# Decode block: gate and up products one step earlier, the MLP's last weights behind the fourth K tile, and half of one head's output weights on 64 partitions

## The chip, the cores and the metric

The kernel runs on one core of one Trainium2 chip; the other cores stand idle. The time is device microseconds of that core for one execution. The core has five engines with instruction streams of their own: TensorE (PE, matmuls; PEld is its weight load), VectorE (DVE), ScalarE (ACT), GpSimd (POOL) and SyncE (SP). SP does no arithmetic here: it issues the transfers from HBM into the on-chip memory (SBUF, 128 partitions), and 16 DMA engines carry them out. A transfer that SP cannot issue yet, because its buffer is still being read, holds up every transfer behind it in SP's stream.

## The reference

One token of a decoder block for a batch of two, in float32: grouped-query attention over a cached context, multiplied by a gated MLP.

```python
# B, D, Hq, Hkv, Sk, Dh, F = 2, 512, 32, 8, 32768, 128, 1792
xn = layernorm(x)                                   # x is (2, 1, 512)
q  = (xn @ wq) as (B, Hq, 1, Dh)
scores = q . k_cache * Dh**-0.5                     # 4 query heads share one K/V head
o  = softmax(scores) . v_cache
s  = o.reshape(B, 1, Hq*Dh) @ wo                    # wo is (4096, 512)
gate, up = xn @ W_gate, xn @ W_up                   # (512, 1792) each
g  = silu((gate * (gate > 0) * up) @ W_down)        # W_down is (1792, 512)
out = x + s * g
```

Each of the two caches holds 2 x 8 x 32768 x 128 floats (268 MB); all weights together are 27.8 MB. Everything is read once.

## The kernel before

**Tiles and steps.** A group is one batch row and one K/V head: 16 groups, ordered head by head with the two batch rows next to each other. A group's 32768 keys are four tiles of 8192 keys (4 MB of K, 4 MB of V each), so there are 64 K tiles, called k0 to k63 here, and 64 steps `s`. In step `s` DVE transposes K tile `s` in four parts (`k_transpose`, tiles named `kts`, buffers from `ktpool`, five of them), PE forms the scores (`scores`, tile `s_...`), and in step `s + 1` DVE copies them out of the accumulators and takes the maximum (`take_scores`, tile `sc`). After a group's fourth tile come the group's maximum (`tile_maximum`, `maximum`) and the exponentials on ACT. Four steps behind the scores, PE reorders the exponentials (`weights`), DVE transposes them (`take_weights`), and in odd steps PE multiplies two tiles with V (`values`, into `o_ps`). Eight steps after a group began, `take_o` and `finish_group` normalise its result; once the second batch row of a head is there, `finish_group` turns the two rows into columns (tile `ots`) by small matmuls that pick rows out of `ob`. Behind the last step `project_near` multiplies the heads 0 to 4 with their part of `wo`, and `project_far` the heads 5 to 7, adds both, multiplies with the MLP's result and adds `x`.

**The MLP.** Its products lie inside the first steps: `mlp_gu` (gate, then up: `ps_g`, `ps_u`) on PE, `mlp_take` and `mlp_h` on DVE, `mlp_down` (`ps_d`) on PE, and the sigmoid-weighted unit on ACT.

**Buffers and the transfer queue.** All large loads go through `load`, that is, through SP's stream, in the order in which the code issues them. Two pools of SBUF receive them. `ring` has two buffers of 32 KB per partition; K tiles take turns in them, and at the end two V tiles and the output weights do. A K tile's buffer is free when its fourth transpose is done. `wide` has one buffer of 64 KB per partition; in turn it holds `wq`, the gate and up weights (`wgu`), the down weights (`wd`), and then pairs of V tiles (`load_vv`, called vv0, vv2, ... here by their first tile). It is free when the last matmul that reads it is done: for `wq` the query projection, for `wgu` the up product, for `wd` the down product, for a V pair the values of both tiles.

**What sets the order.** The tables `extra` (PE work behind a step), `taken` (DVE work within a step) and `ahead` (loads issued behind a step) say in which step a piece stands; the loop over `s` writes each step out, and `pin` ties PE's and DVE's instructions to the order written, while SP issues in the order of the code. Before the loop stand k0, k1, the query projection, and the gate and up weights.

Of the kernel before, what the change touches and what calls it, by code (L numbers as in the profile page):

```python
# [8 lines left out]
F32 = mybir.dt.float32  # L9
# [4 lines left out]
P = 128  # L14
Q = 32
NC = 4
NR = 16
TK = P * NC * NR
SLOTS = 2
NEAR = 5  # L20
ALIGN = 512


@with_exitstack
def kernel(
# [12 lines left out]
    nc = tc.nc  # L38
    B, HKV, SK, DH = kc.shape
    D = x.shape[2]  # L40
# [15 lines left out]
    const = ctx.enter_context(tc.tile_pool(name="const", bufs=1))  # L56
    ktpool = ctx.enter_context(tc.tile_pool(name="ktpool", bufs=5))
    spool = ctx.enter_context(tc.tile_pool(name="spool", bufs=NU + 2))
    work = ctx.enter_context(tc.tile_pool(name="work", bufs=2))
# [25 lines left out]
    n = 1  # L85
# [27 lines left out]
    ots = const.tile([P, HKV, 2, 2, 32], F32, name="ots")  # L113
    nc.vector.memset(ots, 0.0)
    ob = const.tile([64, DH], F32, name="ob")
    nc.vector.memset(ob, 0.0)
    fold = const.tile([P, 32], F32, name="fold")
    nc.vector.reduce_sum(fold, ident.rearrange("p (k m) -> p m k", m=32), axis=AX.X)
    gy = const.tile([P, P], F32, name="gy")
# [4 lines left out]
    KT, VT, ST, KTS, LS, MX, WO = {}, {}, {}, {}, {}, {}, {}  # L124
    SPS, PR, PW = {}, {}, {}

    def load(dst, src):
        nc.sync.dma_start(dst, src)

    def group(g):  # L130
        return g % B, g // B

    def rows_of(src, t, n):
        b, hk = group(t // NU)
        lo = (t % NU) // 2 * 2 * TK
        rows = src[b, hk, lo : lo + 2 * TK, :]
        if n == 2:
            return rows.rearrange("(p r) d -> p (r d)", p=P)
        return rows.rearrange("(p i r) d -> i p (r d)", i=2, p=P)[t % 2]

    def load_one(src, t, name):
        dst = ring.tile([P, NC, NR, DH], F32, tag="r", align_bytes=ALIGN, name=f"{name}_{t}")
        load(dst.rearrange("p c r d -> p (c r d)"), rows_of(src, t, 1))
        return dst
# [7 lines left out]
    def load_vv(t):  # L152
        dst = wide.tile([P, 2, NC, NR, DH], F32, tag="w", align_bytes=ALIGN, name=f"v_{t}")
        load(dst.rearrange("p i c r d -> p (i c r d)"), rows_of(vc, t, 2))
        for i in range(2):
            VT[t + i] = dst[:, i]

    def load_wo(lo, hi):
        w = ring.tile([P, 4, 2, 2, D], F32, tag="r", align_bytes=ALIGN, name=f"wo_{lo}")
        r = REP * DH  # L160
        for hk in range(lo, hi):
            WO[hk] = w[:, hk - lo]
            dst = WO[hk].rearrange("p c i d -> p c (i d)")
            rows = wo[hk * r : (hk + 1) * r, :].rearrange("(c p i) d -> p c (i d)", c=2, i=2)
            if hk < HKV - 1:
                load(dst, rows)
                continue
            load(dst[:, 0], rows[:, 0])
            for i in range(2):
                load(dst[:, 1, i * D : (i + 1) * D], rows[:, 1, i * D : (i + 1) * D])  # L170


    QW = wq.shape[1] // 2
    wqt = wide.tile([P, NKC, 2, QW], F32, tag="w", align_bytes=ALIGN, name="wq")
    load(
# [52 lines left out]
    def load_gu():  # L228
        t = wide.tile([P, 2, NKC, F], F32, tag="w", align_bytes=ALIGN, name="wgu")
        for n, (which, w) in enumerate((("g", wg), ("u", wu))):  # L230
            load(
                t[:, n].rearrange("p k f -> p (k f)"),
                w.rearrange("(p k) f -> p (k f)", k=NKC),
            )
            for k in range(NKC):
                mlp[which, k] = t[:, n, k, :]
# [31 lines left out]
    def load_d():  # L268
        t = wide.tile([P, FI, D], F32, tag="w", align_bytes=ALIGN, name="wd")
        load(t.rearrange("p i d -> p (i d)"), wd.rearrange("(p i) d -> p (i d)", p=P))  # L270
        for i in range(FI):
            mlp["d", i] = t[:, i, :]
# [13 lines left out]


    def k_transpose(t, c):
        part = ktpool.tile([P, NR, 4, Q], F32, tag="kt", name=f"kts_{t}_{c}")
        nc.vector.transpose(  # L290
            part.rearrange("p r e k -> p (r e k)"), KT[t][:, c].rearrange("p r d -> p (r d)")
        )
        KTS.setdefault(t, []).append(part)
# [113 lines left out]
    def finish_group(g):  # L407
        b, hk = group(g)
        if b == 0:
            PO[hk] = ps_m.tile([P, 512], F32, tag="m", name=f"po_{hk}")  # L410
        po, o = PO[hk], OS.pop(g)
        mine = slice(32 * b, 32 * b + REP)
        nc.tensor.matmul(  # L413
            po[mine, :], head, o.rearrange("p c d -> p (c d)"), start=True, stop=True
        )
        nc.vector.reduce_sum(  # L416
            ob[mine, :], po[mine, :].rearrange("p (c d) -> p d c", c=NC), axis=AX.X
        )
        if b < B - 1:
            return  # L420
        PO.pop(hk)
        ob2 = ob.rearrange("p (q i) -> p i q", i=2)
        pick = ident.rearrange("p (b c r) -> p r c b", b=4, r=2)
        for r in range(2):
            for i in range(2):
                nc.tensor.matmul(  # L426
                    po[64 * r : 64 * r + 64, 256 + i * 4 : 260 + i * 4],
                    ob2[:, i, :],
                    pick[:64, r, :2, :B],
                    start=True,  # L430
                    stop=True,
                )
        nc.vector.tensor_copy(
            ots[:, hk, :, :, :B],
            po[:, 256:264].rearrange("p (i c b) -> p c i b", i=2, c=2),
        )

    PY = {}
# [1 line left out]
    def project_near(hks):  # L440
        if not PY:
            PY["near"] = ps_s.tile([P, 512], F32, tag="s", name="py_near")
        for hk in hks:
            w = WO.pop(hk)
            for k in range(4):
                nc.tensor.matmul(  # L446
                    PY["near"][32 * k : 32 * k + 32, :],
                    ots[:, hk, k // 2, k % 2, :],
                    w[:, k // 2, k % 2, :],
                    start=(hk == 0),  # L450
                    stop=(hk == NEAR - 1),
                )
        if hks[-1] == NEAR - 1:
            PY["sb"] = work.tile([P, 4, P], F32, tag="os", name="py_sb")
            nc.vector.tensor_copy(PY["sb"].rearrange("p c n -> p (c n)"), PY["near"])

    def project_far(hks):
        py = ps_s.tile([P, 512], F32, tag="s", name="py")
        parts = [(fold, PY["sb"].rearrange("p c n -> p (c n)"))]
        for hk in hks:  # L460
            w = WO.pop(hk)
            parts += [(ots[:, hk, k // 2, k % 2, :], w[:, k // 2, k % 2, :]) for k in range(4)]
        for n, (o, w) in enumerate(parts):
            for c in range(4):
                nc.tensor.matmul(  # L465
                    py[32 * c : 32 * c + 32, :P],
                    o,
                    w[:, c * P : (c + 1) * P],
                    start=(n == 0),
                    stop=(n == len(parts) - 1),  # L470
                )
        nc.vector.tensor_mul(gy, py[:, :P], gy)
        nc.vector.tensor_add(gy, gy, xy)

    extra, taken, ahead = {}, {}, {}

    def at(where, s, f, *a):
        where.setdefault(s, []).append((f, a))

    END = NK + NU  # L480
    at(ahead, 1, load_d)
    for s in range(NK - 2):
        at(ahead, s, load_k, s + 2)
        if s % 2 and s >= 3:
            at(ahead, s, load_vv, s - 3)
    at(ahead, NK - 2, load_v, NK - 4)
    at(ahead, NK - 1, load_v, NK - 3)
    at(ahead, NK - 1, load_vv, NK - 2)
    at(ahead, NK + 1, load_wo, 0, 4)
    at(ahead, NK + 1, load_wo, 4, HKV)  # L490
    at(extra, 1, mlp_gu, "g")
    at(extra, 1, mlp_gu, "u")
    at(taken, 2, mlp_take, "g")
    at(taken, 2, mlp_take, "u")
    at(taken, 2, mlp_h)
# [28 lines left out]
    for s in range(END + 1):  # L524
        done = s // NU - 2 if s % NU == 0 and s >= 2 * NU else None
        full = s // NU - 1 if 0 < s <= NK and s % NU == 0 else None
        w = s - NU
        if s < NK:
            k_transpose(s, 0)
# [8 lines left out]
        if s < NK:  # L538
            k_transpose(s, 1)
        if full is not None:  # L540
            maximum(full)
        if s < NK:
            k_transpose(s, 2)
        if s == END:
            project_near(range(4))
        if done is not None:
            finish_group(done)
# [7 lines left out]
        if s == END:  # L555
            project_near(range(4, NEAR))
            project_far(range(NEAR, HKV))
        if s % 2 and w > 0:
# [10 lines left out]
    rows = gy.rearrange("(c q) n -> q c n", q=32)  # L569
# [33 lines left out]
```

## Time and profile before

| | |
|---|---|
| median of 3 runs | 1330.86 us (1330.72 to 1330.94) |
| the profiled execution's own time | 1330.93 us |
| its span, first to last instruction | 1329.1 us |
| PE, PEld, DVE, ACT busy | 908.2, 216.8, 707.1, 52.1 us |
| HBM read | 564.67 MB, 425 GB/s over the span |
| mean granted TensorE clock | 0.836 |

The profile is one execution. Its page gives the busy time of each engine, the span in 40 slices of 33 us with the share of time in which the 16 DMA engines were busy, the chain of work that ended last, and the costliest groups of instructions. Further views are the timeline (instructions with start and duration in us and, in brackets, how long the engine had been idle and what released it), tables by stretches of time, and who waited for whom. A DMA row of the timeline (SPq) is the issue on SP, not the transfer; a row that joins several issues has the start of the first.

### The profile page before, as it was taken

To read this page: it belongs to the slowest core of one execution; us is meant where nothing else is said; L and a number is where in the kernel's file an instruction comes from. 1 tells how busy PE (TensorE), PEld (TensorE's weight loads), DVE (VectorE), ACT (ScalarE), POOL (GpSimd) and SP (SyncE) were. 2 spreads that over 40 slices of the span, in tenths; PEclk is the share of its full clock that TensorE was granted. 3 is DMA by queue.
4 is the path that set the end of the run, shared out by engine and by line. 5 is a ranking of instruction groups with operands and counts; after the bars stand their busy time and mean duration, and the time that the engine had idled before them with its cause. 6 is when DMAs were issued, how large, how long until landed. Compare 5 with 4: busy or idle time off the path is not lost.

```text
span 1329.1 us, 10685 instructions
## 1 busy us (share of the span) xinstructions
PE 908.2 (68%) x4736; PEld 216.8 (16%) x4736; DVE 707.1 (53%) x667; ACT 52.1 (4%) x136; POOL 0.7 (0%) x6
## 2 busy tenths in 40 slices
PE   3586667776775776767568676757767676776775
PEld 1121111121111111111111111112111111111112
DVE  3848445466644546656454665545466554546610
ACT  0001000000000000000000000000000000000000
POOL 0000000000000000000000000000000000000000
PEclk9799788878878887878897778888889777987887
DMA  9979999999999999999999999999999999999997
GB/s 411 427 314 411 440 415 423 440 427 439 436 438 427 432 427 436 431 442 438 426 428 431 435 432 438 432 440 424 430 432 437 439 428 438 430 427 431 444 429 307
DMA packets 16962, 565.36 MB, mean 425 GB/s; under 512 B 1794, under 2 KB 1810, under 8 KB 3988
## 3 DMA queue, kind: packets, MB, share of 16 engines
q1 hardware_dynamic: 16888, 564.67, 98.6%
q8 instruction: 37, 0.61, 0.2%
q14 instruction: 9, 0.07, 0.0%
q10 hardware_dynamic: 28, 0.01, 0.0%
HBM read 564.67 MB, written 0.00 MB: 425 GB/s over the span
## 4 chain that ended last, share of the span: by engine, by line
DMA 66%; DVE 26%; PE 7%; issue 1%; DVEq 0%
DMA k<-in_A_k_cache_dram 60%; DVE kts L290 21%; DMA v<-in_A_v_cache_dram 5%; PE s L302 2%; PE o_ps L374 2%; DMA wq<-in_A_wq_dram 2%; DVE sc L316 1%; DVE os L396 1%; DVE ob L416 1%; PE pr L344 1%; PE pq L201 1%; DVE qt L220 0%; PE po L426 0%; PE py_near L446 0%; PE py L465 0%
## 5 line engine op out<-in xcount | busy, mean ns | idle before, releaser
L290 DVE STREAM_TRANSPOSE kts<-k 128x2048 f32<-128x2048 f32 x256 | 578.0, 2287 | 462.8 <-DMA k<-in_A_k_cache_dram 462.8
L302 PE MATMUL s<-kts,qt 128*32 128x512 f32 x2048 | 490.0, 729 | 186.6 <-DVE kts L290 183.3
L374 PE MATMUL o_ps<-v,sc 128*16 128x512 f32 x2048 | 258.7, 646 | 80.3 <-DMA v<-in_A_v_cache_dram 80.3
L302 PEld LDWEIGHTS s<-kts,qt 128*32 128x32 f32 x2048 | 97.0, 128 | 579.0 <-DVE kts L290 322.2
L374 PEld LDWEIGHTS o_ps<-v,sc 128*16 128x16 f32 x2048 | 62.4, 102 | 255.8 <-issue 167.1
L352 ACT ACTIVATE sc<-sc,nb 128x512 f32<-128x512 f32 x64 | 45.4, 710 | 1130.4 <-DVE nb L348 1130.4
L358 PE MATMUL pt<-sc,perm 128*128 128x512 f32 x128 | 85.4, 757 | 1.3 <-ACT sc L352 1.3
L316 DVE TENSOR_SCALAR_CACHE_REDUCE sc<-s 128x512 f32<-128x512 f32 x64 | 43.1, 673 | 58.9 <-PE s L302 58.9
L330 PE MATMUL pr<-ident,m 128*1 128x128 f32 x16 | 5.2, 327 | 79.3 <-DVE m L328 79.3
L367 DVE STREAM_TRANSPOSE sc<-pt 128x512 f32<-128x512 f32 x64 | 43.3, 676 | 12.7 <-PE pt L358 12.4
L344 PE MATMUL pr<-negone,mrow 1*128 1x1 f32 x32 | 8.9, 344 | 33.4 <-DVE mrow L341 33.4
L358 PEld LDWEIGHTS pt<-sc,perm 128*128 128x128 f32 x128 | 22.0, 215 | 54.1 <-issue 39.2
L413 PE MATMUL po<-os,head 128*4 128x512 f32 x32 | 28.2, 982 | 0.0
L394 DVE RECIPROCAL rl<-pl 128x1 f32<-128x1 f32 x16 | 2.6, 164 | 26.4 <-PE pl L389 26.4
L330 PEld LDWEIGHTS pr<-ident,m 128*1 128x1 f32 x16 | 1.3, 79 | 94.0 <-DVE m L328 92.1
L396 DVE SCALAR_TENSOR_TENSOR os<-o_ps,rl,own 128x512 f32<-128x512 f32 x16 | 12.0, 751 | 8.3 <-PE o_ps L374 6.8
L344 PEld LDWEIGHTS pr<-negone,mrow 1*128 1x128 f32 x32 | 7.5, 290 | 37.4 <-DVE mrow L341 37.4
L201 PE MATMUL pq<-wq,xt 128*32 128x512 f32 x64 | 8.8, 715 | 6.7 <-DMA wq<-in_A_wq_dram 6.7
L416 DVE TENSOR_REDUCE ob<-po 4x128 f32<-4x512 f32 x16 | 10.6, 662 | 4.5 <-PE po L413 4.3
L277 PE MATMUL ps_d<-wd,ht 128*32 128x512 f32 x28 | 12.2, 592 | 0.0
L352 ACT ACTIVATION_READ_ACCUMULATOR sc<-sc,nb 128x1 f32 x64 | 11.9, 186 | 0.0
L426 PE MATMUL po<-ident,ob 64*64 64x4 f32 x64 | 4.6, 244 | 10.5 <-DVE ob L416 10.5
(74 smaller groups left out, 107.6 us busy)
## 6 DMA issues: line engine op xcount, KB each, us to landing
k<-in_A_k_cache_dram SPq DMA_DIRECT2D x64, 4096.0 KB, 26.7
v<-in_A_v_cache_dram SPq DMA_DIRECT2D x2, 4096.0 KB, 29.5
wo<-in_A_wo_dram SPq DMA_DIRECT2D x7, 1024.0 KB, 17.7
wgu<-in_B_W_gate_dram SPq DMA_DIRECT2D x1, 3584.0 KB, 19.9
wgu<-in_B_W_up_dram SPq DMA_DIRECT2D x1, 3584.0 KB
wd<-in_B_W_down_dram SPq DMA_DIRECT2D x1, 3584.0 KB
wo<-in_A_wo_dram SPq DMA_DIRECT2D x1, 512.0 KB
wo<-in_A_wo_dram SPq DMA_DIRECT2D x2, 256.0 KB
```

Of the source, the lines that this page charges most:

```text
L201: nc.tensor.matmul(pq[half][32 * c : 32 * c + 32, :], xn[:, k, :], wqt[:, k, half, c * 512 : (c + 1) * 512], start=(k == 0), stop=(k == NK ...
L290: nc.vector.transpose(part.rearrange("p r e k -> p (r e k)"), KT[t][:, c].rearrange("p r d -> p (r d)"))
L302: nc.tensor.matmul(ps[Q * c : Q * c + Q, :], qt[:, b, hk, e, :], kts[c][:, :, e, :], start=(e == 0), stop=(e == 3),)
L316: nc.vector.tensor_scalar(ST[t].rearrange("p r m -> p (r m)"), SPS.pop(t), SCALE, None, op0=ALU.mult, op1=ALU.max, accum_out=MX[g][:, u : ...
L344: nc.tensor.matmul(pr[:, 256:257], mrow.rearrange("o c k h -> o (c k h)"), negone, start=True, stop=True)
L352: nc.scalar.activation(st, st, AF.Exp, bias=nbias, scale=1.0, accum_out=LS[g][:, u : u + 1])
L358: nc.tensor.matmul(PW[t], perm.rearrange("p k c h -> p (k c h)"), ST[t].rearrange("p r m -> p (r m)"), start=True, stop=True,)
L367: nc.vector.transpose(ST[t].rearrange("p r m -> p (r m)"), PW.pop(t))
L374: nc.tensor.matmul(ops[g % 2][a : a + NC * REP, :, :], w[:, r, : NC * REP], v[:, :, r, :], start=(u == 0 and r < 4), stop=(u == NU - 1 and ...
L396: nc.vector.scalar_tensor_tensor(OS[g], ops[g % 2], rl, own.unsqueeze(2).to_broadcast([P, NC, DH]), op0=ALU.mult, op1=ALU.mult,)
L413: nc.tensor.matmul(po[mine, :], head, o.rearrange("p c d -> p (c d)"), start=True, stop=True)
L416: nc.vector.reduce_sum(ob[mine, :], po[mine, :].rearrange("p (c d) -> p d c", c=NC), axis=AX.X)
```

## The change

Three edits and their consequences:

- `mlp_gu` for gate and up stands behind step 0 instead of step 1, so PE has both products ahead of the scores of k1.
- `load_d` (the down weights) stays in step 1, but behind the load of k3 instead of ahead of it. What followed in SP's stream keeps its order.
- Head 6's output weights (`LOW = 6`), 1 MB, are loaded in three transfers instead of one: the first half as before into 128 partitions, the second half as two transfers of 256 KB into the partitions 0 to 31 and 32 to 63 of a `ktpool` buffer (`wo_low`, 8 KB per partition). `finish_group` for that head makes a rearranged copy of `ob` (`obl`) and eight small matmuls into a new tile `otl` (64 partitions); `project_far` uses four products of 64 partitions there in place of two of 128. The `ktpool` tiles get an alignment of 512 bytes.

```diff
@@ load_wo
+            if hk == LOW:
+                load(dst[:, 0], rows[:, 0])
+                WO["low"] = ktpool.tile([P, 4, D], F32, tag="kt", align_bytes=ALIGN, name="wo_low")
+                flat = WO["low"].rearrange("p j d -> p (j d)")
+                for h in range(2):
+                    a = hk * r + (2 + h) * P
+                    load(
+                        flat[32 * h : 32 * h + 32, :],
+                        wo[a : a + P, :].rearrange("(a e j) d -> e a (j d)", a=4, e=8),
+                    )
+                continue
             if hk < HKV - 1:
                 load(dst, rows)
@@ k_transpose
-        part = ktpool.tile([P, NR, 4, Q], F32, tag="kt", name=f"kts_{t}_{c}")
+        part = ktpool.tile([P, NR, 4, Q], F32, tag="kt", align_bytes=ALIGN, name=f"kts_{t}_{c}")
@@ finish_group
+        n = 1 if hk == LOW else 2
...
+        if hk != LOW:
+            return
+        obl = work.tile([P, NC, DH], F32, tag="os", name="obl")[:64, 0].rearrange(
+            "p (j x) -> p j x", j=4
+        )
+        nc.vector.tensor_copy(
+            obl.rearrange("p j (e a) -> p j e a", a=4),
+            ob.rearrange("p (a e j) -> p j e a", a=4, e=8),
+        )
+        for h in range(2):
+            for j in range(4):
+                nc.tensor.matmul(
+                    po[32 * h : 32 * h + 32, 320 + j * B : 320 + (j + 1) * B],
+                    obl[:, j, :],
+                    pick[:64, h, 1, :B],
+                    start=True,
+                    stop=True,
+                )
+        nc.vector.tensor_copy(
+            otl[:, :, :B], po[:64, 320 : 320 + 4 * B].rearrange("p (j b) -> p j b", j=4)
+        )
@@ project_far
-            parts += [(ots[:, hk, k // 2, k % 2, :], w[:, k // 2, k % 2, :]) for k in range(4)]
+            n = 2 if hk == LOW else 4
+            parts += [(ots[:, hk, k // 2, k % 2, :], w[:, k // 2, k % 2, :]) for k in range(n)]
+            if hk == LOW:
+                parts += [(otl[:, j, :], WO["low"][:64, j, :]) for j in range(4)]
@@ tables of the loop
-    at(ahead, 1, load_d)
     for s in range(NK - 2):
         at(ahead, s, load_k, s + 2)
+        if s == 1:
+            at(ahead, s, load_d)
...
-    at(extra, 1, mlp_gu, "g")
-    at(extra, 1, mlp_gu, "u")
+    at(extra, 0, mlp_gu, "g")
+    at(extra, 0, mlp_gu, "u")
```

**Where it moves instructions.** On SP, early in the program, before: `k_306` is k2, `k_372`, `k_428` and `k_457` are k3, k4 and k5, `wd` the down weights, `v_459` the pair vv0.

```order
L128 DMA wgu<-in_B_W_up_dram 128x7168
L128 DMA k_306<-in_A_k_cache_dram 128x8192
L128 DMA wd<-in_B_W_down_dram 128x7168
L128 DMA k_372<-in_A_k_cache_dram 128x8192
L128 DMA k_428<-in_A_k_cache_dram 128x8192
L128 DMA k_457<-in_A_k_cache_dram 128x8192
L128 DMA v_459<-in_A_v_cache_dram 128x16384
```

The same place in the changed kernel, where `k_342`, `k_372`, `k_430` and `k_459` are k2 to k5 and `v_461` is vv0:

```order
L131 DMA wgu<-in_B_W_up_dram 128x7168
L131 DMA k_342<-in_A_k_cache_dram 128x8192
L131 DMA k_372<-in_A_k_cache_dram 128x8192
L131 DMA wd<-in_B_W_down_dram 128x7168
L131 DMA k_430<-in_A_k_cache_dram 128x8192
L131 DMA k_459<-in_A_k_cache_dram 128x8192
L131 DMA v_461<-in_A_v_cache_dram 128x16384
```

k3 and `wd` have changed places. On PE, around the gate and up products, before (`s_319` are the scores of k1, `s_392` those of k2, `kts_0_...` to `kts_3_...` the four transposed parts of a tile):

```order
L302 MATMUL s_319<-kts_2_315,qt 32x512
L302 MATMUL s_319<-kts_3_317,qt 32x512
L242 MATMUL ps_g<-wgu,xt 32x448 x16
L242 MATMUL ps_u<-wgu,xt 32x448 x16
L302 MATMUL s_392<-kts_0_374,qt 32x512
L302 MATMUL s_392<-kts_1_386,qt 32x512
```

In the changed kernel, where `s_291` are the scores of k0 and `s_355` those of k1:

```order
L316 MATMUL s_291<-kts_2_287,qt 32x512
L316 MATMUL s_291<-kts_3_289,qt 32x512
L256 MATMUL ps_g<-wgu,xt 32x448 x16
L256 MATMUL ps_u<-wgu,xt 32x448 x16
L316 MATMUL s_355<-kts_0_344,qt 32x512
L316 MATMUL s_355<-kts_1_349,qt 32x512
```

Both products now stand ahead of the scores of k1. On PE at the program's end, before (`py_near` and `py` are the accumulators of the two projections):

```order
L446 MATMUL py_near<-wo_3889,ots 32x512 x16
L413 MATMUL po_3848<-os_3945,head 4x512
L426 MATMUL po_3848<-ident,ob 64x4 x4
L446 MATMUL py_near<-wo_3894,ots 32x512 x4
L465 MATMUL py<-py_sb,fold 32x128 x4
L465 MATMUL py<-wo_3894,ots 32x128 x48
```

And in the changed kernel:

```order
L482 MATMUL py_near<-wo_3902,ots 32x512 x16
L427 MATMUL po_3861<-os_3961,head 4x512
L441 MATMUL po_3861<-ident,ob 64x4 x4
L482 MATMUL py_near<-wo_3907,ots 32x512 x4
L504 MATMUL py<-py_sb,fold 32x128 x4
L504 MATMUL py<-wo_3907,ots 32x128 x24
L504 MATMUL py<-wo_low,otl 32x128 x16
L504 MATMUL py<-wo_3907,ots 32x128 x16
```

The far projection has 56 products of weights instead of 48; the trace counts each float32 product as two instructions, 96 before.

More of the change, by code (lines that the diff above doesn't have):

```diff
@@ L20 @@
 NEAR = 5
+LOW = 6
 ALIGN = 512
@@ L116 @@
     nc.vector.memset(ob, 0.0)
+    otl = const.tile([64, 4, 32], F32, name="otl")
+    nc.vector.memset(otl, 0.0)
     fold = const.tile([P, 32], F32, name="fold")
@@ L426, in finish_group @@
                 nc.tensor.matmul(
-                    po[64 * r : 64 * r + 64, 256 + i * 4 : 260 + i * 4],
+                    po[64 * r : 64 * r + 64, 256 + i * n * B : 256 + (i + 1) * n * B],
                     ob2[:, i, :],
-                    pick[:64, r, :2, :B],
+                    pick[:64, r, :n, :B],
                     start=True,
@@ L433, in finish_group @@
         nc.vector.tensor_copy(
-            ots[:, hk, :, :, :B],
-            po[:, 256:264].rearrange("p (i c b) -> p c i b", i=2, c=2),
+            ots[:, hk, :n, :, :B],
+            po[:, 256 : 256 + 2 * n * B].rearrange("p (i c b) -> p c i b", i=2, c=n),
+        )
[19 more added lines that the diff above has]
+            otl[:, :, :B], po[:64, 320 : 320 + 4 * B].rearrange("p (j b) -> p j b", j=4)
         )
```

## The prediction

> **What bounds the kernel now.** I read the page first: busy times, the DMA and GB/s rows of the slices, and the queue that carries the loads.
>
> ```profile
> PE 908.2 (68%) x4736; PEld 216.8 (16%) x4736; DVE 707.1 (53%) x667; ACT 52.1 (4%) x136; POOL 0.7 (0%) x6
> DMA  9979999999999999999999999999999999999997
> GB/s 411 427 314 411 440 415 423 440 427 439 436 438 427 432 427 436 431 442 438 426 428 431 435 432 438 432 440 424 430 432 437 439 428 438 430 427 431 444 429 307
> q1 hardware_dynamic: 16888, 564.67, 98.6%
> k<-in_A_k_cache_dram SPq DMA_DIRECT2D x64, 4096.0 KB, 26.7
> wd<-in_B_W_down_dram SPq DMA_DIRECT2D x1, 3584.0 KB
> ```
>
> No compute engine is near full, and the DMA engines are: 98.6% of their time goes into the load queue. Only two slices fall below 411 GB/s, the third (66 to 100 us) and the last. A K tile waits 26.7 us from issue to landing. Next I read the table by stretches; its last columns are the granted clock, the DMA share and GB/s.
>
> ```profile
> 60.00:65.00 5.00, 3.83 (x4) 0.36 (x4) 5.00 (x3) 0.00 (x0) 0.00 (x0) 0.54 0.99 426
> 65.00:70.00 5.00, 4.89 (x40) 1.56 (x44) 0.41 (x2) 0.00 (x0) 0.00 (x0) 0.78 0.50 216
> 70.00:75.00 5.00, 5.00 (x58) 2.87 (x50) 3.17 (x4) 0.00 (x0) 0.00 (x0) 1.00 0.01 3
> 75.00:80.00 5.00, 0.79 (x5) 0.00 (x0) 4.11 (x5) 0.00 (x0) 0.00 (x0) 1.00 0.73 264
> 105.00:110.00 5.00, 3.62 (x26) 0.90 (x26) 3.60 (x3) 0.00 (x0) 0.00 (x0) 1.00 0.61 216
> 160.00:1240.00 1080.00, 752.38 (x3838) 175.10 (x3830) 587.81 (x508) 41.01 (x112) 0.00 (x0) 0.83 1.00 433
> ```
>
> From 160 to 1240 us the share is 1.00 at 433 GB/s: in the long middle nothing but bytes sets the pace, and each microsecond in which the DMA engines stand idle is added to the end. They stood idle 2.5 + 4.95 + 1.35 = 8.8 us around 68 to 77 us and 1.95 us around 106 us, together 10.75 us. The timeline of SP's issues, of DVE and of PE says why.
>
> ```profile
> 51.23 0.33 SPq L128 DMA_DIRECT2D k<-in_A_k_cache_dram  x1
> 57.75 0.69 DVE L316 TENSOR_SCALAR_CACHE_REDUCE sc<-s 128x512 f32<-128x512 f32 x1 [4.36 <-PE s L302]
> 58.37 6.69 DVE L290 STREAM_TRANSPOSE kts<-k 128x2048 f32<-128x2048 f32 x3
> 65.11 4.23 PE L302 MATMUL s<-kts,qt 128*32 128x512 f32 x25 [0.28 <-DVE kts L290]
> 69.65 2.31 DVE L290 STREAM_TRANSPOSE kts<-k 128x2048 f32<-128x2048 f32 x1 [4.59 <-DMA k<-in_A_k_cache_dram]
> 71.88 0.65 DVE L316 TENSOR_SCALAR_CACHE_REDUCE sc<-s 128x512 f32<-128x512 f32 x1
> 72.52 2.52 PE L242 MATMUL ps_u<-wgu,xt 128*32 128x448 f32 x24
> 75.82 0.33 SPq L128 DMA_DIRECT2D wd<-in_B_W_down_dram  x1
> 75.83 0.62 DVE L253 COPY sb_u<-ps_u 128x448 f32<-128x448 f32 x1 [2.38 <-PE ps_u L242]
> 76.25 30.16 SPq L128 DMA_DIRECT2D k<-in_A_k_cache_dram  x3
> 78.54 6.66 DVE L290 STREAM_TRANSPOSE kts<-k 128x2048 f32<-128x2048 f32 x3
> 88.29 11.75 PE L277 MATMUL ps_d<-wd,ht 128*32 128x512 f32 x27
> 106.50 0.38 SPq L128 DMA_DIRECT2D v<-in_A_v_cache_dram  x1
> 109.77 0.69 DVE L316 TENSOR_SCALAR_CACHE_REDUCE sc<-s 128x512 f32<-128x512 f32 x1 [1.17 <-PE s L302]
> 118.25 11.41 SPq L128 DMA_DIRECT2D k<-in_A_k_cache_dram  x2
> 138.79 8.79 PE L374 MATMUL o_ps<-v,sc 128*16 128x512 f32 x64 [5.80 <-DMA v<-in_A_v_cache_dram]
> 147.65 0.33 SPq L128 DMA_DIRECT2D v<-in_A_v_cache_dram  x1
> 148.49 2.31 DVE L290 STREAM_TRANSPOSE kts<-k 128x2048 f32<-128x2048 f32 x1 [18.58 <-DMA k<-in_A_k_cache_dram]
> 1197.67 2.31 DVE L290 STREAM_TRANSPOSE kts<-k 128x2048 f32<-128x2048 f32 x1 [16.91 <-DMA k<-in_A_k_cache_dram]
> ```
>
> k2 is issued at 51.23 and is there at 69.65. The next issue, `wd`, goes out at 75.82, when the up product has freed the wide buffer, and k3 stands behind it (76.25) although its own buffer was free at 58.37 + 6.69 = 65.06, when k1's transposes ended. So the queue ran dry. It ran dry again at 106: the third issue of the row at 76.25 is k5, which ended that row at 106.4 and waited for k3's transposes, late because k3 was late.
>
> **What the gaps are worth.** k6 reaches DVE at 148.49, k60 at 1197.67. In between lie 27 periods of two K tiles and a V pair, 108 tiles: 1049.18 / 108 = 9.715 us a tile with the queue never empty. Between k2 (69.65) and k6 (148.49) the queue carried `wd` (3584/4096 = 0.875 tile), k3 to k6 and a V pair, 6.875 tiles, which take 66.79 us at that pace. It took 78.84. The excess is 12.05 us; the idle shares explain 10.75 of it, and the rest I put down to restarting from empty.
>
> **Edits to the loads and the MLP.** With k3 first, SP issues it at 65.1, 4.5 us before k2 lands, and no longer waits for PE there. What is queued behind, at one tile per 9.715 us from 69.65: k3 lands at 79.4, `wd` at 87.9, k4 at 97.6, k5 at 107.3, vv0 at 126.7, k6 at 136.5, k7 at 146.2. Each next issue must come before its predecessor lands.
>
> - `wd` waits for the up product. PE is free for gate and up when the scores of k0 are out (57.75); the up weights are there one tile before k2, by 59.9. The 24 matmuls of the row at 72.52 took 2.52 us at clock 1.00, so all 64 take 6.7 us, at the 0.54 of the stretch 60 to 65 us 12.4. Done at 64 to 70; needed by 79.4. Queued behind on PE are k1's scores, on SP k4.
> - k4 waits for k2's transposes. DVE does the first by 71.96, then takes k1's scores (0.65). These are ready 4.23 us after k1's last transpose by the row at 65.11, at 69.3; if PE is held by the MLP until 70.1 and all 32 matmuls follow, at 75.6. Then come the five MLP steps, 2.7 us from 75.83 to 78.54 and 0.6 for the gate copy, without the 2.38 us wait, and three transposes (6.66): issue at 82.6 to 86.2, against 87.9. Before it was 85.2.
> - k5 waits for k3's transposes: on DVE from 82.6, the first done by 84.9, k2's scores ready 4.2 us after k2's last transpose and taken by 87.5, three more transposes: 94.2, against 97.6.
> - vv0 waits for the down product, 12.2 us (11.75 for 27 of its 28 instructions) from `wd`'s landing: 100.1, against 107.3. At this place PE now waits for `wd`, about 2 us, and k3's scores stand behind it.
> - k6: k3's scores end at about 104.3; before, k6 left 8.48 us after that point (109.77 to 118.25): 112.8, against 126.7. vv2 follows the values of vv0, 8.8 us after its landing: 135.6, against 146.2. That is the 10 us of backlog it had before (147.65).
>
> Every margin is positive, the smallest 1.7 to 5.3 us (k4) and 3.4 us (k5). I take the whole 12.05 us. A transfer needs a moment from issue to its first bytes, and the scores too may run at a low clock, so that up to 2 us can come back at k4.
>
> **Head 6, in the middle.** In step 60 come two DVE copies, eight small products (16 instructions) and a wait of DVE for PE ahead of the last transpose.
>
> ```profile
> 1207.91 0.60 PE L426 MATMUL po<-ident,ob 64*64 64x4 f32 x8 [1.38 <-DVE ob L416]
> 1208.57 0.17 DVE L433 COPY ots<-po 128x8 f32<-128x8 f32 x1 [0.71 <-PE po L426]
> 1210.99 12.88 SPq L128 DMA_DIRECT2D k<-in_A_k_cache_dram  x2
> v<-in_A_v_cache_dram SPq DMA_DIRECT2D x31, 30.3
> ```
>
> Twice the 0.60 us, since there are twice as many, less the overlap, and two copies of 0.17 to 0.3: an estimate of 1.2 us by which k62's issue (1210.99) is later. The cover is the backlog: a K tile lands 26.7 us after its issue, 17 of them behind others, a V pair 30.3 for 19.4 of its own. Cost zero; 1.2 us if there were no backlog. The memset of `otl` lies in DVE's wait for `x` at the start, and the alignment adds no instruction: zero.
>
> **Head 6, at the end.** All of it hangs on the last V pair.
>
> ```profile
> 1305.21 5.83 PE L374 MATMUL o_ps<-v,sc 128*16 128x512 f32 x32 [12.16 <-DMA v<-in_A_v_cache_dram]
> 1322.43 2.94 PE L465 MATMUL py<-wo,ots 128*32 128x128 f32 x96
> 1324.94 0.16 PEld L465 LDWEIGHTS py<-wo,ots 128*32 128x32 f32 x8 [0.19 <-DMA wo<-in_A_wo_dram]
> 1320.00:1322.00 2.00, 1.37 (x16) 0.44 (x16) 0.73 (x2) 0.00 (x0) 0.00 (x0) 1.00 0.57 235
> 1283.33 28.47 SPq L128 DMA_DIRECT2D wo<-in_A_wo_dram  x10
> ```
>
> From the landing of the last V pair PE runs to the end with one wait for weights, 0.19 us. Sixteen more instructions at 2.94/96 = 31 ns cost 0.5 us, and the wait can vanish: +0.3. The share of 0.57 says that about nine of the sixteen DMA engines are still busy when the others are done, so the last weights belong to late engines. If the 512 KB move from late engines to early ones, the last landing comes earlier and nothing more is gained than the 0.19. If they move onto the late ones, they take 2.4 us at half of 433 GB/s instead of 1.2, the last landing is 1.2 us later and the end with it. So -0.2 to +1.2. I take +0.3, since the instructions are certain and no row tells the late engines from the early. SP's two more issues cost nothing: ten went out by 1311.8, and two more at the 0.33 us of a single issue are out before the weights ahead of them have moved.
>
> [...]
>
> **Sum.** The profiled execution took 1330.93 us, 0.07 above the median. 1330.93 - 12.05 + 0.3 = 1319.2 us.
>
> **The rivals.**
> - Part of the gap comes back: k4, k5 or vv0 misses its moment, because PE with the MLP in front is late under a low clock. For it speaks the 0.54 just where the products now stand; against it that DVE loses its 2.38 us wait. Price 2 to 5 us: 1321 to 1324.
> [...]
> - Slower: not bytes but the turnaround of the two ring buffers sets the steady pace. Then the early gain is swallowed by a later wait, and what head 6 adds stays: 1.2 in step 60, 0.5 for instructions, 1.2 for the landing, 2.9 in all, 1333.8. It decides once the backlog at an issue is under 1.2 us; the 1.00 share over 1080 us speaks against it.
> - The reorder does nothing, because k3 is not ready to go before the up product either: about 1331. Against it stands 65.06 from the transposes.
>
> **How the numbers follow.** Forecast with its tail bounds, 1318.6 to 1320.5, including the rival of the eight late engines (0.15 of it): 0.77. Part of the gap back: 0.16. Slower: 0.03. No effect: 0.03. The rest, 0.01, is a gain beyond the excess. To hold 8 in 10 the range goes from 1318.0, a little under the bound of the excess (1330.93 - 12.05 - 0.2 = 1318.7), to 1322.5, halfway into the partial case. About 0.2% (2.7 us) is what a measurement of this kernel can tell from no change: faster 0.94, same 0.03, slower 0.03.
>
> **What would show it.** Right: DMA share near 1.00 in all stretches from 65 to 130 us, k3 issued at 65, `wd` at 64 to 70, k6 on DVE at about 136.5 instead of 148.5, the last V pair's values 12 us earlier, and the same length from there to the end but for 0.3. Wrong: a stretch with a low share between 80 and 110 us (k4, k5 or vv0 late), a pace above 9.715 us a tile later on, or a longer wait for `wo` in the far projection.

## The result and the profile after

The changed kernel takes 1320.59 us in the median of 6 runs (1319.75 to 1323.00), the kernel before 1330.9 (1330.07 to 1332.61): a ratio of 0.9923 with an interval of 0.9911 to 0.9936. So it is faster, by 0.8%. The profiled execution took 1319.75 us, and its span is 1318.0 us. The forecast was 1319.2, in a range of 1318.0 to 1322.5.

From the page of the changed kernel, the DMA row of the slices and the load queue:

```profile
DMA  9999999999999999999999999999999999999997
q1 hardware_dynamic: 16840, 564.67, 99.3%
```

The third slice is full (7 before) and the queue takes 99.3% of the DMA engines' time (98.6% before) for the same 564.67 MB. The table by stretches, with the granted clock, the DMA share and GB/s at the end (a packet counts in the stretch in which it starts, so a short stretch can show a share above 1):

```profile
65.00:78.00 13.00, 5.28 (x28) 0.92 (x20) 7.98 (x9) 0.00 (x0) 0.00 (x0) 0.79 1.01 434
90.00:100.00 10.00, 10.00 (x30) 2.57 (x29) 5.97 (x3) 0.00 (x0) 0.00 (x0) 1.00 0.99 406
104.00:109.00 5.00, 0.90 (x4) 0.62 (x4) 4.26 (x8) 0.92 (x3) 0.00 (x0) 0.76 1.11 478
65.00:130.00 65.00, 46.96 (x207) 11.11 (x203) 43.08 (x35) 5.28 (x13) 0.00 (x0) 0.84 1.00 426
160.00:1240.00 1080.00, 747.65 (x3860) 173.24 (x3852) 588.94 (x511) 41.01 (x112) 0.00 (x0) 0.84 1.00 433
```

Both gaps are closed, and none has opened around 95 us, where the queue, which now runs some 10 us earlier, could have run dry. The middle runs as before. The timeline of the changed kernel, SP's issues first, then rows of PE and DVE:

```profile
52.17 12.90 SPq L131 DMA_DIRECT2D k<-in_A_k_cache_dram  x2
65.25 0.33 SPq L131 DMA_DIRECT2D wd<-in_B_W_down_dram  x1
82.69 11.35 SPq L131 DMA_DIRECT2D k<-in_A_k_cache_dram  x2
100.31 0.33 SPq L131 DMA_DIRECT2D v<-in_A_v_cache_dram  x1
112.49 11.76 SPq L131 DMA_DIRECT2D k<-in_A_k_cache_dram  x2
135.98 0.33 SPq L131 DMA_DIRECT2D v<-in_A_v_cache_dram  x1
60.23 3.21 PE L256 MATMUL ps_u<-wgu,xt 128*32 128x448 f32 x32
86.38 0.69 DVE L330 TENSOR_SCALAR_CACHE_REDUCE sc<-s 128x512 f32<-128x512 f32 x1 [1.52 <-PE s L316]
88.10 11.75 PE L291 MATMUL ps_d<-wd,ht 128*32 128x512 f32 x27 [1.76 <-DMA wd<-in_B_W_down_dram]
97.72 2.31 DVE L304 STREAM_TRANSPOSE kts<-k 128x2048 f32<-128x2048 f32 x1 [4.03 <-DMA k<-in_A_k_cache_dram]
137.06 2.31 DVE L304 STREAM_TRANSPOSE kts<-k 128x2048 f32<-128x2048 f32 x1 [12.57 <-DMA k<-in_A_k_cache_dram]
1187.02 2.31 DVE L304 STREAM_TRANSPOSE kts<-k 128x2048 f32<-128x2048 f32 x1 [16.03 <-DMA k<-in_A_k_cache_dram]
```

In the first row two issues are grouped, k2 at 52.17 and k3, which ends the group at 65.07; `wd` follows at once, since the up product ends at 63.4. In the same way k5 goes out at the end of the row at 82.69, at 94.0, and k4 reaches DVE at 97.72. k6 reaches DVE at 137.06, 11.43 us earlier than before (148.49), k60 at 1187.02, 10.65 earlier. The pace between them is (1187.02 - 137.06) / 108 = 9.722 us a tile, against 9.715.

The end of the program, on PE, PE's weight loads and DVE's part of step 60:

```profile
1197.93 0.16 DVE L448 COPY ots<-po 128x4 f32<-128x4 f32 x1 [0.71 <-PE po L441]
1199.17 0.16 DVE L470 COPY otl<-po 64x8 f32<-64x8 f32 x1 [0.91 <-PE po L463]
1293.52 5.73 PE L388 MATMUL o_ps<-v,sc 128*16 128x512 f32 x32 [12.26 <-DMA v<-in_A_v_cache_dram]
1310.64 1.49 PE L504 MATMUL py<-wo,ots 128*32 128x128 f32 x48
1312.06 1.08 PE L504 MATMUL py<-wo_low,otl 64*32 64x128 f32 x32
1313.07 1.40 PE L504 MATMUL py<-wo,ots 128*32 128x128 f32 x32
1314.04 0.16 PEld L504 LDWEIGHTS py<-wo,ots 128*32 128x32 f32 x8 [0.38 <-DMA wo<-in_A_wo_dram]
```

The last V pair's product starts 11.69 us earlier than before (1305.21). From there to the end of the span it is 24.48 us, against 23.9 before. So 11.7 us were gained up to the last V pair and 0.6 went back at the end; the two profiled executions differ by 11.2.

### The profile page after: what moved, and what is told of

It reads as the page before. It is cut to its first block, busy times and chain, and to the rows that moved or that the text cites. A ratio compares the mean times of both kernels' runs of the same rounds, so it can differ in the third digit from the quotient of the medians.

```text
span 1318.0 us, 10755 instructions
## 1 busy us (share of the span) xinstructions
PE 899.1 (68%) x4768; PEld 214.6 (16%) x4768; DVE 707.3 (54%) x670; ACT 52.1 (4%) x136; POOL 0.7 (0%) x6
## 3 DMA queue, kind: packets, MB, share of 16 engines
q1 hardware_dynamic: 16840, 564.67, 99.3%
HBM read 564.67 MB, written 0.00 MB: 428 GB/s over the span
## 4 chain that ended last, share of the span: by engine, by line
DMA 67%; DVE 25%; PE 6%; issue 1%; SPq 0%; DVEq 0%; ACT 0%; ACTq 0%
DMA k<-in_A_k_cache_dram 59%; DVE kts L304 21%; DMA wo<-in_A_wo_dram 3%; DMA v<-in_A_v_cache_dram 2%; DMA wd<-in_B_W_down_dram 2%; DMA wq<-in_A_wq_dram 2%; PE s L316 1%; DVE sc L330 1%; PE o_ps L388 1%; PE ps_d L291 1%; DVE os L410 1%; PE pr L358 1%; PE pq L215 1%; DVE ob L430 1%; DVE qt L234 0%
## 5 line engine op out<-in xcount | busy, mean ns | idle before, releaser
L316 PE MATMUL s<-kts,qt 128*32 128x512 f32 x2048 | 483.5, 721 | 190.3 <-DVE kts L304 187.1
L388 PE MATMUL o_ps<-v,sc 128*16 128x512 f32 x2048 | 253.3, 634 | 77.8 <-DMA v<-in_A_v_cache_dram 77.8
L441 PE MATMUL po<-ident,ob 64*64 64x4 f32 (+1 forms) x64 | 4.6, 244 | 10.5 <-DVE ob L430 10.5
```

The costliest lines, as they stand in the source:

```text
L316: nc.tensor.matmul(ps[Q * c : Q * c + Q, :], qt[:, b, hk, e, :], kts[c][:, :, e, :], start=(e == 0), stop=(e == 3),)
L388: nc.tensor.matmul(ops[g % 2][a : a + NC * REP, :, :], w[:, r, : NC * REP], v[:, :, r, :], start=(u == 0 and r < 4), stop=(u == NU - 1 and ...
```

## The experiments

**The theory:** the gain is the closing of the two gaps of the load queue, by the two edits together; head 6 adds nothing to it. The first four runs have each edit of the start alone, both of them without head 6, and head 6 alone.

*k3 ahead of `wd`, and nothing else.* On the kernel before:

```
-    at(ahead, 1, load_d)
     for s in range(NK - 2):
         at(ahead, s, load_k, s + 2)
+        if s == 1:
+            at(ahead, s, load_d)
```

> The kernel before with one edit: k3's load ahead of the down weights; gate and up stay behind the scores of k1. Theory (the transfer queue only has to hold something at all times): k3 goes out at 65, the down weights still at 76 when the up product is done, which is 3 us before k3 lands, so the queue never runs dry; k4 as before at 85, ahead of the landing of the down weights at 88. About 1319 us, the whole 11 to 12 us of the change. Rival 1 (the early products do the work, because they free the wide buffer): k3 alone ahead gains only its own tile, about 1327 to 1329. Rival 2 (each edit brings a share): about 1325.

Measured: 1323.01 us, ratio 0.9935 (0.9920 to 0.9949). The theory's 1319 is missed by 4 us. The table by stretches of this kernel and its timeline:

```profile
65.00:78.00 13.00, 11.06 (x92) 4.37 (x84) 5.37 (x8) 0.00 (x0) 0.00 (x0) 0.87 1.02 434
90.00:100.00 10.00, 10.00 (x26) 2.53 (x23) 7.87 (x6) 0.00 (x0) 0.00 (x0) 1.00 0.89 354
76.09 0.33 SPq L128 DMA_DIRECT2D wd<-in_B_W_down_dram  x1
85.49 13.05 SPq L128 DMA_DIRECT2D k<-in_A_k_cache_dram  x2
90.87 0.69 DVE L316 TENSOR_SCALAR_CACHE_REDUCE sc<-s 128x512 f32<-128x512 f32 x1 [3.22 <-PE s L302]
99.44 2.31 DVE L290 STREAM_TRANSPOSE kts<-k 128x2048 f32<-128x2048 f32 x1 [1.26 <-DMA k<-in_A_k_cache_dram]
```

The first gap is closed. The second stays, only smaller and earlier: k5 goes out at the end of its row, 85.49 + 13.05 = 98.5, still ahead of k4's arrival on DVE (99.44), and yet the queue runs dry. The packet records of this trace (each DMA packet with its start, duration and size) show why. Fifteen of the sixteen engines had run out of k4's packets between 97.0 and 98.9 us, and the first packets of k5 come at 99.2, 0.95 us after its issue began at 98.2. With the MLP products still behind k1's scores, k2's transposes are done 2.8 us later than in the changed kernel (k4 at 85.49, not 82.69), and DVE waits 3.22 us for k2's scores instead of 1.52, so that k5 is 4.5 us later.

*The products early, and nothing else.*

```
-    at(extra, 1, mlp_gu, "g")
-    at(extra, 1, mlp_gu, "u")
+    at(extra, 0, mlp_gu, "g")
+    at(extra, 0, mlp_gu, "u")
```

> The kernel before with the other edit: gate and up behind the scores of k0; the down weights stay ahead of k3. Theory: the down weights go out at about 64, k3 at 65, so the gap at 68 to 77 us closes here too; but k3 lands one transfer later (88 instead of 79), its transposes end at about 97, just when k4 has landed, so that the gap of 1.7 us idle and its restart, about 2.3 us, stays: 1321 us. Rival 1 (the early products do all): 1319. Rival 2 (each edit a share): about 1325.

Measured: 1322.62 us, ratio 0.9934 (0.9918 to 0.9951). The theory had the right gap and 1321 us, 1.6 too few. Its stretches and SP's issues:

```profile
65.00:78.00 13.00, 4.81 (x24) 0.79 (x16) 8.14 (x9) 0.00 (x0) 0.00 (x0) 0.76 1.02 437
90.00:100.00 10.00, 10.00 (x47) 3.28 (x47) 9.74 (x7) 2.34 (x5) 0.00 (x0) 1.00 0.71 285
63.35 0.33 SPq L128 DMA_DIRECT2D wd<-in_B_W_down_dram  x1
64.27 33.51 SPq L128 DMA_DIRECT2D k<-in_A_k_cache_dram  x3
```

Here `wd` goes out at 63.35 and k3 behind it, so the first gap is closed too. But k3 lands a transfer later than in the changed kernel (`wd` is 0.875 of a K tile), its transposes are late, and k5, the last of the row at 64.27, goes out at 97.8 with the queue empty again. Either edit alone is worth 8.4 to 8.8 us, both are worth 10 to 11: they close the same first gap, and only together the second (share 0.89 and 0.71 from 90 to 100 us, 0.99 in the changed kernel).

*Both, without head 6* (LOW, `otl`, `wo_low` and the alignment of `kts` left as before).

> Both edits of loads and MLP, head 6 as before. Theory: the length from the first product with the last V pair to the end is 23.9 us as before and not the 24.5 us of the change, so about 0.6 us faster than the change: 1319 us by the profile of the change (1319.75), 1320 by its median. Rival (head 6's new place brings the end forward): 0.5 to 1 us slower than the change.

Measured: 1320.22 us, ratio 0.9915 (0.9900 to 0.9930). The changed kernel, run again as a control, gave 1320.41, ratio 0.9921 (0.9905 to 0.9938). The 0.6 us that leaving out head 6 was to bring came out as 0.2, less than the spread of either:

> The changed kernel once more, beside the next ones on the same chip: about 1320.5 us, k6 on DVE at about 137, 24.2 to 24.8 us from the first product with the last V pair to the end. All theories expect the same.

*Head 6 alone* (the tables of the loop as before, the rest as changed).

> Head 6's weights on partitions 0 to 63 alone, loads and MLP as before. Theory: both gaps of the queue stay; the end is 0.3 to 1.2 us longer after the last V pair: 1331.2 to 1332.1, the same as before by measurement. Rival (the small loads take work off the late DMA engines, which end last): 0.2 to 1.2 us faster, 1329.7 to 1330.7.

Measured: 1332.12 us against 1331.38, ratio 1.0005 (0.9996 to 1.0015): no change. All of the gain is the start. The last V product with both edits and without head 6, in the repeated changed kernel, and with head 6 alone:

```profile
1294.46 6.10 PE L374 MATMUL o_ps<-v,sc 128*16 128x512 f32 x32 [12.11 <-DMA v<-in_A_v_cache_dram]
```
```profile
1294.56 5.60 PE L388 MATMUL o_ps<-v,sc 128*16 128x512 f32 x32 [12.41 <-DMA v<-in_A_v_cache_dram]
```
```profile
1306.29 6.22 PE L388 MATMUL o_ps<-v,sc 128*16 128x512 f32 x32 [12.11 <-DMA v<-in_A_v_cache_dram]
```

With the spans 1318.4, 1318.6 and 1330.9 us, the ends take 23.9 us without head 6 and 24.0 and 24.6 with it (23.9 before, 24.5 in the first trace of the changed kernel): head 6 costs 0.1 to 0.7 us at the end.

*DVE later by five copies a step.* On the changed kernel, ahead of the last transpose of each step:

```
+            for _ in range(5):
+                nc.vector.tensor_copy(idle, qt[:, 0, :4].rearrange("p h e q -> p (h e q)"))
             k_transpose(s, 3)
```

> The changed kernel with five more copies of 128 x 512 on DVE ahead of the last transpose of every step (they write a tile that nothing reads), an estimate of 2.1 us by the 0.42 us of such a copy: each K load is issued 2.1 us later. Theory (bytes set the steady pace, the backlog of 10 to 17 us covers the issue): the middle keeps its 9.7 us a tile; only at the start, where the margins of k4 and k5 are 2 to 5 us, a gap of 1 to 2 us opens near 97 us, so 2 to 3 us slower than the change, 1322 to 1324. Rival (the turnaround of the two ring buffers sets the pace): 64 steps of 2.1 us, up to 134 us slower.

Measured: 1328.70 us, ratio 0.9979 (0.9969 to 0.9990), 8.3 us slower than the changed kernel beside it, where 2 to 3 were expected.

```profile
65.00:78.00 13.00, 6.97 (x48) 1.88 (x40) 9.93 (x14) 0.00 (x0) 0.00 (x0) 0.87 0.75 306
100.00:110.00 10.00, 9.01 (x45) 2.26 (x43) 6.90 (x10) 2.35 (x5) 0.00 (x0) 1.00 0.55 216
160.00:1240.00 1080.00, 770.15 (x3848) 170.26 (x3841) 701.12 (x785) 41.02 (x112) 0.00 (x0) 0.80 1.00 432
146.43 2.31 DVE L305 STREAM_TRANSPOSE kts<-k 128x2048 f32<-128x2048 f32 x1 [11.20 <-DMA k<-in_A_k_cache_dram]
```

DVE is busy 112 us more in the middle, and the queue does not notice: the share is 1.00 at 432 GB/s. So the slower rival of the prediction, that the turnaround of the two ring buffers sets the steady pace, falls. At the start the same delay costs 8 us: both gaps are back (shares 0.75 and 0.55), and k6 reaches DVE 9.4 us later. The expectation counted the delay of a step once. But the copies of steps 0 to 3 add up along the chain of buffers: the trace has k3's issue at 70.6 us, 5.5 later than in the changed kernel, and k5's at 104.3, 10.3 later, more than the margins there.

*Which engines carry the small loads.* A probe on the kernel before: four loads of 128 KB, 8 rows outermost as in the change, behind k2, where the queue then runs dry (the tile `spare` and the other tables are left out here).

```
+    def probe():
+        flat = spare.rearrange("p j d -> p (j d)")
+        for h in range(4):
+            load(flat[32 * h : 32 * h + 32, :],
+                 wo[64 * h : 64 * h + 64, :].rearrange("(a e j) d -> e a (j d)", a=4, e=8))
...
+    at(ahead, 0, load_k, 2)
+    at(ahead, 0, probe)
```

> The kernel before, with four loads of 32 partitions and 128 KB each, 8 rows outermost, behind k2, where the queue runs dry afterwards. Nothing reads them. Theory: they run on eight engines, so after k2 the DMA share stands near 0.5 for 2.4 us (512 KB at half of 433 GB/s). Rival (all sixteen): near 1.0 for 1.2 us, then nothing.

Measured: 1331.23 us. Some rows of the table by stretches of 1 us:

```profile
66.00:67.00 1.00, 1.00 (x12) 0.23 (x8) 0.00 (x0) 0.00 (x0) 0.00 (x0) 0.50 0.83 360
68.00:69.00 1.00, 1.00 (x12) 0.24 (x8) 0.00 (x0) 0.00 (x0) 0.00 (x0) 0.92 0.48 197
69.00:70.00 1.00, 1.00 (x16) 0.53 (x12) 0.01 (x1) 0.00 (x0) 0.00 (x0) 1.00 0.48 197
71.00:72.00 1.00, 1.00 (x16) 0.61 (x12) 1.00 (x1) 0.00 (x0) 0.00 (x0) 1.00 0.07 29
```

For two microseconds the share is half and the rate is about half. A share of 0.48 could also be sixteen engines that each work half of the time; the packet records exclude that. At 67 us sixteen packets are in flight, from 68.4 to 70.2 eight or nine, and each of the small ones (4 KB) takes 159 ns, as those of the output weights do in the kernel before. So with 8 outermost these loads went over eight engines, each at its usual speed.

*32 rows outermost instead.* The changed kernel with the two low loads written with 32 rows outermost (and `obl` in the order that fits):

```
-                        wo[a : a + P, :].rearrange("(a e j) d -> e a (j d)", a=4, e=8),
+                        wo[a : a + P, :].rearrange("(e j) d -> e (j d)", j=4),
```

> The changed kernel, the two small loads of head 6 read with 32 rows outermost instead of 8 (the copy obl rearranged to match). Theory (8 outermost confines a load to eight engines, some of them the late ones): with 32 all sixteen engines share them, the DMA share 14 us after the last V pair is 0.63 and below as in the kernel before, not 0.88; the last weights come 0.8 us earlier after the last V pair than in the change, and the end 0.2 to 0.4 us earlier. Rival (the partitions, not the pattern, decide the engines): the same stretch as in the change, 0.88.

Measured: 1324.01 us, ratio 0.9946 (0.9931 to 0.9961): 3.6 us slower than the changed kernel beside it, where a little faster was expected. The start is the same; the end, on PE, with a stretch of the DMA engines of this kernel, and the same stretch of the changed one behind it:

```profile
1293.56 5.01 PE L388 MATMUL o_ps<-v,sc 128*16 128x512 f32 x32 [13.80 <-DMA v<-in_A_v_cache_dram]
1314.88 1.08 PE L504 MATMUL py<-wo_low,otl 64*32 64x128 f32 x32 [1.90 <-DMA wo_low<-in_A_wo_dram]
1304.00:1306.00 2.00, 2.00 (x21) 0.54 (x14) 0.00 (x0) 0.00 (x0) 0.00 (x0) 1.00 1.01 289
```
```profile
1304.00:1306.00 2.00, 2.00 (x24) 0.57 (x17) 0.00 (x0) 0.00 (x0) 0.00 (x0) 1.00 0.94 375
```

The DMA engines are no less busy with 32 outermost (1.01 against 0.94) and move less (289 GB/s against 375), so the transfers themselves are slower. From 1303 to 1304 us the rate is 209 GB/s at a share of 1.03, about half of the steady 433; a half is also what the theory of the next probe takes. The 64 packets of 8 KB that bring the low weights take 460 ns on average, against 309 in the changed kernel, and PE waits 1.90 us for these weights. Three more probes look for what slows them.

*The same bytes into other partitions.* On the kernel before, in each of steps 10 to 49 a load of 384 KB into a tile that nothing reads, 64 rows outermost; `LO` is 0 in the first kernel and 32 in the second (the tile `spare` is left out):

```
+    def probe(s):
+        a = 192 * (s % 16)
+        load(spare[LO : LO + 64].rearrange("p j d -> p (j d)"),
+             wo[a : a + 192, :].rearrange("(e j) d -> e (j d)", j=3))
...
+        if 10 <= s < 50:
+            at(ahead, s, probe, s)
```

> The kernel before, with a load of 384 KB into partitions 0 to 63 (64 rows outermost, 6 KB each; nothing reads it) behind the K tile of each of steps 10 to 49, 40 in all, 15.73 MB. At the steady 433 GB/s they take 36.3 us, at half of it 72.6. Theory (a load into partitions 0 to 63 is taken at about half the full rate, whatever the number of engines): 1331 + 73 = 1404, with the share staying at 1.00 and the rate over these steps falling to 433 * (4.19 + 0.39) / (4.19 + 0.79) = 398 GB/s. Rival (rows next to each other in memory are what slowed the sixteen-engine loads): 1404 here too, and also for partitions 32 to 95. Rival (the slow packets were a matter of the tail only): 1367.

> The same as with partitions 0 to 63, but into partitions 32 to 95: the same bytes, rows and engines. Theory (which partitions are written decides; these lie on both sides of partition 64): full rate, 1331 + 36 = 1367. Rival (rows in memory, or the number of partitions): 1404, as with 0 to 63.

Measured, one execution each: 1482.96 us into partitions 0 to 63 and 1369.29 us into 32 to 95, with 1331.10 before. The second costs 0.95 us a load, where the bytes alone cost 0.91 at 433 GB/s. The first costs 152 us, 3.8 a load. A stretch of each, partitions 0 to 63 first (the 40 loads go out between 237 and 1152 us there, and between 237 and 1041 us in the second kernel):

```profile
700.00:1100.00 400.00, 256.05 (x1218) 55.14 (x1214) 180.81 (x155) 11.73 (x32) 0.00 (x0) 0.78 0.97 384
```
```profile
700.00:1100.00 400.00, 270.07 (x1349) 62.06 (x1349) 206.53 (x180) 14.66 (x40) 0.00 (x0) 0.82 1.00 433
```

Bytes, rows in memory and sizes are the same, and in the code only the partitions written differ, so these decide (1482.96 against 1369.29 us; how many engines carried the loads was not counted); the rivals (neighbouring rows, the number of partitions) fall. At half of 433 GB/s those bytes alone would take 1.8 us a load, and 3.8 were measured. The theory's 398 GB/s left out the V tile that each step also loads; with it half the rate gives (8.39 + 0.39) / (8.39 + 0.79) of 433, that is 414, and 384 was measured. The packet records say where the rest goes. A packet of a probe (6 KB) takes 234 ns into 32 to 95 and 398 ns on average into 0 to 63. The 32 KB packets, nearly all of them of K tiles, take 1291 ns on average instead of 1216, and the 64 KB packets, nearly all of V pairs, 2503 instead of 2424. Summed over sixteen engines, the 152 us are about 37 for the bytes of the probes at the undisturbed 234 ns, 26 for their own slowness, 60 for that of the packets around them, and 28 in which engines stood idle. So the tiles in flight pay more than the probes do. Why a packet into partitions 0 to 63 takes longer was not shown.

*8 rows outermost into partitions 0 to 63, in the stream.* The same 40 loads with 8 outermost:

```
-             wo[a : a + 192, :].rearrange("(e j) d -> e (j d)", j=3))
+             wo[a : a + 192, :].rearrange("(a e j) d -> e a (j d)", a=8, e=8))
```

> The same 40 loads into partitions 0 to 63, but with 8 outermost in the source, so that eight engines carry them. Theory (eight engines at their full speed, the other eight idle or ahead): each of the eight has 48 KB more a step, 1.8 us at 27 GB/s, and every K tile waits for the slowest engine: 1331 + 73 = 1404, with a share below 1.00 (about (9.7 + 0.9) / (9.7 + 1.8) = 0.92). Rival (the number of engines does not matter): 1367 at a share of 1.00.

Measured, one execution: 1555.62 us, 5.6 a load.

```profile
700.00:1100.00 400.00, 233.94 (x1100) 49.68 (x1100) 170.32 (x146) 11.72 (x32) 0.00 (x0) 0.76 0.93 347
```

That is slower than the rival, and the share is below 1.00, as the theory had it (0.92; with the V tile of each step 0.96), but the price is three times the theory's. By the packet records the 224 us are about 37 for the bytes, 23 for the slowness of the probes' packets (378 ns on average), 99 for that of the packets around them, and 65 of idle engines. Why the tiles in flight suffer more than with 64 rows outermost was not found. So eight outermost is no better form as such: in the middle of the stream it is the dearest of the three. At the end of the changed kernel, where each load writes 32 partitions, it costs 0.1 to 0.7 us, and 32 outermost cost some 3 us more.

## Why the prediction was right

- *The middle is bound by bytes, so each idle microsecond is added to the end.* Right: 1.00 and 433 GB/s again, and 112 us more of DVE work there did not change it.
- *The two gaps are worth 12.05 us.* Nearly: the last V product came 11.69 us earlier, k6 11.43, k60 10.65. The term is 0.4 to 1.4 too big, the tail adds a few tenths in the same direction, and the difference of the medians is 10.3. What was too much is the 1.3 us that the prediction put down to restarting from empty. With the gaps closed, the four traces with both edits still take 67.1 to 68.4 us from k2 to k6 on DVE, against 66.79 at the steady pace, and the changed kernel moves 426 GB/s, not 433, from 65 to 130 us at a share of 1.00. So most of that part was no cost of the gaps.
- *Each next issue comes before its predecessor lands.* The times are right, to within 0.6 us: `wd` 65.25 (64 to 70), k4 82.69 (82.6 to 86.2), k5 94.0 (94.2), vv0 100.31 (100.1), k6 112.49 (112.8), vv2 135.98 (135.6), `wd` at PE 88.10 (87.9), k4 on DVE 97.72 (97.6), k6 on DVE 137.06 (136.5). The low clock that made k4's margin doubtful did not come where the products now stand: the up product's 32 instructions took 3.21 us, and the granted clock from 60 to 65 us was 1.00, against 0.54 before. The rival of a part that comes back did not happen. As a condition, though, it is too weak: with the load order alone k5 went out 0.9 us ahead of k4's arrival on DVE, and the queue ran dry. By the packet records a transfer's first packets come 0.95 us after its issue (k5 there, `wd` and k5 before), and the first engine is out of work 1.2 to 2.5 us before DVE sees the tile. Added up, an estimate of the lead that is needed is 2 to 3.5 us. In the changed kernel k5 has 3.7, and the 1.7 us that the prediction allowed for k4 at worst might not have been enough.
- *What the two edits do apart* was not in the prediction, and the first expectation had it wrong: the order of the loads alone was to bring all of it. It leaves the second gap, because k5's margin (94.0 against 97.7) is made by the products' earlier place.
- *Step 60 costs nothing.* The estimate of 1.2 us was 1.2: `otl` is copied 1.24 us after `ots`. Hidden: head 6 alone is 1.0005.
- *The tail costs 0.3.* It took 0.6 in the profiled execution, 0.1 to 0.7 over all of them, inside the bounds of -0.2 to +1.2. The wait of 0.19 did not vanish; it is 0.38 at the same place.
- *The eight engines.* The 0.15 that the forecast gave to small loads on eight engines that end late rested on no run or row. The probe shows the eight: with 8 rows outermost eight or nine packets are in flight, at a share of 0.48 and 197 GB/s. Whether the eight are the late ones was not settled. What the prediction did not see at all is that the partitions written matter: a packet of 6 KB took 398 ns into 0 to 63 and 234 into 32 to 95. It had no effect on the sum because the two small loads, as the change writes them, cost 0.1 to 0.7 us at the end; with 32 rows outermost they cost some 3 us more.
- *The reorder does nothing* falls with k3's issue at 65.07; *slower* falls with the copies on DVE.
- *The band.* The bounds of the sum, -0.2 to +1.2 around 1318.9, give 1318.7 to 1320.1, and the text says 1318.6 to 1320.5 at 0.77. The median of 1320.59 lies just above both and below the 1321 to 1324 of a gap that comes back; the range has it because it was drawn wider, while the mechanism is the one that was forecast.

## What to carry to other kernels

Where one queue's bytes set the end, look for the stretches in which its share falls below one, find for each the issue that came late and what the issuing engine stood waiting for, and price the gap by the pace of the full queue. Check every later issue against the landing of the one before it, with some 3 us to spare by the traces here: closing a gap moves the next shortage, and two edits that each seem enough can be needed together. Don't place a big load on partitions 0 to 63 without measuring it: the same bytes into 32 to 95 were four times cheaper (0.95 us for 384 KB against 3.8; 64 to 127 was not tried).

## What the hardware showed that was not expected

A load into partitions 0 to 63 with 64 rows outermost slowed the whole stream: 3.8 us for 384 KB, against 0.95 into partitions 32 to 95, with the DMA share at 0.97 and the rate at 384 GB/s instead of 433. Most of it was paid by the K and V packets around the load and by idle engines (60 and 28 of the 152 us), not by the slowness of the load's own packets (26). A share near 1.00 therefore doesn't say that the bytes move at full speed; share and GB/s are to be read together. And the same bytes with 8 rows outermost cost 5.6 us a load in the full stream, while at its end head 6 with two loads of 8 rows outermost, 512 KB in all and 32 partitions each, cost 0.1 to 0.7 us.
